# A two-layer decode kernel: another load order and other buffer places where a layer ends, and the output projection in pieces

## The chip, the cores and the metric

The kernel runs on one core of a Trainium2 chip. Its time is device microseconds of that core, from runs of the compiled program; the figure for the kernel before is the median of 10 runs. One further execution was taken with the hardware profiler; everything read from a profile or a trace here is from that one.

The engines' short names are those of the profile: PE is the matrix engine (its matmuls; PEld its weight loads), DVE the vector engine, ACT the scalar engine, SP the engine whose queue issues all loads. Sixteen DMA engines carry the loads.

## What is computed

```python
def _A_ref(x, k_cache, v_cache, wq, wo):          # B=2, one token, D=576, H=32, Sk=16384, Dh=128
    q = (x @ wq).reshape(B, Sq, H, Dh).transpose(0, 2, 1, 3)
    scores = einsum("bhqd,bhkd->bhqk", q, k_cache) * (Dh ** -0.5)
    p = softmax(scores, axis=-1)
    o = einsum("bhqk,bhkd->bhqd", p, v_cache)
    return o.transpose(0, 2, 1, 3).reshape(B, Sq, H * Dh) @ wo
...
x = A_x
x = x + _A_ref(_layernorm(x), k_cache, v_cache, wq, wo)
x = x + _B_ref(_layernorm(x), w1, w2, w3, w4)
x = x + _A_ref(_layernorm(x), k_cache, v_cache, wq, wo)
x = x + _B_ref(_layernorm(x), w1, w2, w3, w4)
```

`_B_ref` is a small MLP block: with one token its shifted branch leaves `x1 = x` (a product with zeros), and then `x1 + gelu(layernorm(x1) @ w3) @ w4`, with w3 of 576 x 4608 and w4 of 4608 x 576. Everything is bf16. Both layers read the same caches, 64 pairs of batch and head with 4 MB of K and 4 MB of V each: more than 1 GB in all, against a few MB of weights per layer.

## The kernel before

**Units.** A unit is one pair of batch and head. A layer is 64 units, then the MLP. Layer 1 takes the units in the order 0 to 63, layer 2 in the reverse, so that the last two units of layer 1 are the first two of layer 2 and stay in SBUF (`N_KEEP`, `kept`). In this document K[i] and V[i] are those of the i-th unit *in the order of the layer*, and "unit i" is that unit.

**A unit's work** (`attention`, L790). The K tile lies with 128 rows of the cache per column group. Half of it, in eight turns (`turn`, L656), is transposed by PE, copied out by ACT, and multiplied with the query on PE (`score`, L675). The other half is done by DVE: a product with the query's rows and a sum, eight pairs (`dots`, L687; L694 and L697). `row_max` and `unit_max` (L702, L712) give the maximum, `exps` (L720) the weights on ACT, and `weigh` (L731) is V times the weights on PE, 64 matmuls for each half of V. It runs one unit late: unit i's V is weighed inside unit i+1, around the end of its turns. PE's program has a loop over most units (`loops`, L796), with a body of two units: units 2 to 57 of layer 1 and 6 to 57 of layer 2; the others are written out.

**Places.** One SBUF tensor `buf` is cut in three thirds ("places" 0, 1, 2); a third has room for one K and one V (16384 bf16 per partition each). `place` (L328) tells which third a unit uses. In layer 1 units alternate between thirds 0 and 1; unit 63 uses third 2. In layer 2 the first five use 2, 0, 1, 2, 0, and from unit 5 on they alternate: odd units third 1, even ones third 2. The third that isn't used by units (2 in layer 1, 0 in layer 2) takes `wo`, in seven pieces of four heads and one "middle" piece of three heads (`want_wo`, L396); the last head has a tile of its own, `wolast`. wq for layer 1, and w2, use third 2 too; w3 and w4 use third 1 in layer 1 (that of unit 61) and third 0 in layer 2; wq for layer 2 comes into third 1, behind layer 1's w3 and w4.

**The queue of loads.** `plan` (L335) writes down all loads once, in one order: K[i], then V[i-1], from layer 2's unit 5 on as in layer 1; for layer 2's first five units K[i] and V[i] together. At the end come K[63], V[62], V[63], w3 in five row blocks and w4 in four pieces (`want_w34`, L375). The pieces of w4 have 5, 4, 2 and 1 parts; the first lies behind w3, the other three lie over w3's rows, so they wait until w3's matmuls have read them:

```python
                if c == 1:
                    at = base
```

`Arena` (L190) keeps this order. SP issues the loads one after the other, and each waits until the readers of what lay at its place are done. So K[i+2] waits for the dots of unit i where two thirds alternate, and a load that waits holds up all behind it.

**The output projection** (`project`, L748). For a range of heads: the softmax denominators by a matmul with ones, their sum and reciprocal on DVE, the normalized outputs `otn`, then one group of matmuls per head with `wo`, and a DVE add into `xa`. At the start of unit 59 the seven large pieces are projected in one go (140 matmuls), in layer 1 behind `shift_term` (L625); the middle piece at the end of unit 62, the last head after unit 63:

```python
            if i == last + 1:
                if l == 0:
                    self.shift_term()
                self.project_pieces(l, range(self.n_wo - 1))
```

PSUM tile `misc` is shared by these steps, the query rows and the unit maximum; `ops` has the result of weigh.

Of the kernel before, what the change touches and what calls it, by code (L numbers as in the profile page):

```python
# [4 lines left out]
ALU = mybir.AluOpType  # L5
# [228 lines left out]
class Decode:  # L234
# [2 lines left out]
    NKT = 3  # L237
    N_KEEP = 2
    N_MID = 3
    WO_PIECE = 4  # L240
    FJ = 3
    W4_PIECES = (5, 4, 2, 1)
# [85 lines left out]
    def place(self, l, i):  # L328


        if l == 0:
            return 2 if i == self.U - 1 else i % 2
        return (2, 0, 1, 2, 0)[i] if i < 5 else (2, 1)[i % 2]

    def plan(self):  # L335
        ring, B, H, D, KT, U = self.ring, self.B, self.H, self.D, self.KT, self.U
        unit = 2 * self.half
        self.order = [list(range(U)), list(reversed(range(U)))]
        self.kept = set(self.order[0][-self.N_KEEP:])

        def kv(kind, l, i, split=False):
            u = self.order[l][i]
            if l == 1 and u in self.kept:
                return
            b, hh = u % B, u // B
            src = {"K": self.K, "V": self.V}[kind][b, hh]
            pl = self.place(l, i)
            at = pl * self.place_n + {"K": 0, "V": unit}[kind]
            if split:
                ap = src.rearrange("(t p j) d -> t p (j d)", t=2, p=128)  # L350
                for h in range(2):
                    ring.want([(kind, l, u, h)], at + h * self.half, self.half,
                              [lambda e, v, h=h: e.dma_start(v, ap[h])])
            else:
                ap = src.rearrange("(p j) d -> p (j d)", p=128)
                ring.want([(kind, l, u, h) for h in range(2)], at, unit, [lambda e, v: e.dma_start(v, ap)],
                          sem=f"{kind}{pl}")
# [13 lines left out]

        def want_wq(l, p):
            rows("wq", l, self.wq, p * self.place_n + unit, last=p * self.place_n + 7 * unit // 8)

        def want_w34(l, p):  # L375
            base = p * self.place_n
            rows("w3", l, self.w3, base)
            at, a0 = base + (2 * KT - 1) * self.F // 2, 0
            for c, n in enumerate(self.W4_PIECES):
                m = n * self.FJ * D  # L380
                if c == 1:
                    at = base
# [3 lines left out]
                ring.want([("w4", l, c)], at, m,  # L386
                          [lambda e, v, ap=ap, n=n: e.dma_start(v.rearrange("p (a m) -> p a m", a=n), ap)])
# [13 lines left out]

        want_wq(0, 2)
        for l in range(2):
            wp = 2 - 2 * l
            early = 5 if l == 1 else 0
            gap = max(1, (U - 16) // self.n_wo)
            for i in range(U):
                kv("K", l, i, split=(l == 1 and i == 2))
                if i < early:
                    kv("V", l, i)  # L410
                elif i - 1 >= early:
                    kv("V", l, i - 1)
                j, r = divmod(i - 7, gap)
                if r == 0 and 0 <= j < self.n_wo:
                    want_wo(l, j, wp * self.place_n + (unit if j == self.n_wo - 1 else j * self.WO_PIECE * D))
                if l == 0 and i == 6:
                    want_w2(wp * self.place_n + 5 * unit // 4)
# [313 lines left out]
    def weigh(self, l, i, h):  # L731
        u = self.order[l][i]
        q = i % 2
        vt, res = self.ring.get(self.key("V", l, u, h))

        def f(pe):
            for j in range(self.TB):
                ins = pe.matmul(self.ops[q][:, 0:1], lhsT=vt[:, j * 128:(j + 1) * 128],  # L738
                                rhs=self.p[q][:, h * self.TB + j:h * self.TB + j + 1],
                                start=(h == 0 and j == 0), stop=(h == 1 and j == self.TB - 1))  # L740
            return ins
        self.pe(f, r=[*res, f"p{q}"], w=[f"P:ops{q}"])
        self.release("V", l, u, h)
        if h == 1:
# [3 lines left out]
    def project(self, l, h0, h1, parts):  # L748


        B, D, KT = self.B, self.D, self.KT
        u0, u1 = h0 * B, h1 * B
# [8 lines left out]
        self.dve(lambda v: v.tensor_tensor(out=self.otn[:, u0:u1], in0=self.o[:, u0:u1], in1=den, op=ALU.mult),  # L761
                 r=["den", "o"], w=["otn"])
        out = self.misc[:, 256:256 + KT * B]
        for first, n, w, res, after in parts:
            def f(pe, first=first, n=n, w=w):
                for j in range(n):
# [7 lines left out]
                                           in1=out.rearrange("p (t b) -> p t b", b=B), op=ALU.add),  # L774
                 r=["P:misc", "xa"], w=["xa"])

    def project_pieces(self, l, js):
# [6 lines left out]
        self.project(l, parts[0][0], parts[-1][0] + parts[-1][1], parts)  # L784

    def project_last(self, l):
        h = self.order[l][-1] // self.B
        self.project(l, h, h + 1, [(h, 1, self.wolast[:, :], ["wolast"], lambda: None)])

    def attention(self, l):  # L790
        U, NCP, NCH = self.U, self.NCP, self.NCH
        self.waiting = []
        self.query(l, 0)
        self.query_rows(l, 0)
        first, last = 2 + 4 * l, U - 6
        self.s.loops.append((l * U + first, (last - first) // 2, 2))  # L796
        for i in range(U):
            self.s.tag = l * U + i
            if i == U // 2:
                self.load_wo_last(l)  # L800
# [20 lines left out]
            while self.waiting:  # L821
                self.score()
            if i >= 1:
                self.weigh(l, i - 1, 1)
            if i == U - 2:
                self.project_pieces(l, [self.n_wo - 1])
            if i + 1 < U:
                self.query_rows(l, i + 1)
            self.row_max(l, i)
        self.s.tag = None  # L830
        self.unit_max(l, U - 1)
# [37 lines left out]
```

## Time and profile before

| | |
|---|---|
| median of 10 runs | 2591.03 us (2590.16 to 2591.62) |
| the profiled execution's own time | 2591.68 us |
| its span, first to last instruction | 2589.9 us |
| DVE busy | 1977.2 us, 76% |
| PE busy | 1537.1 us, 59% |
| ACT busy | 1110.2 us, 43% |
| HBM read | 1097.74 MB, 424 GB/s over the span |
| mean granted PE clock | 0.656 |

The page gives busy time, not need: an engine that waits for data isn't busy. Times inside the execution count from the span's start. A line such as L694 is a line of the kernel; the line of a load is that of the lambda which made it (L356: a whole K or V, L353: half of one, L370: rows of wq or w3, L387: a piece of w4, L400: a piece of wo). The page has a row per group of instructions, a row per group of loads with its size and the median time from issue to landing, and slices of the span; the trace gives the same for any stretch. A load has landed when all sixteen DMA engines have carried their share.

### The profile page before, as it was taken

What the parts mean: (1) busy time and instruction counts of PE and PEld (TensorE: products, weight loads), DVE (VectorE), ACT (ScalarE), POOL (GpSimd) and SP (SyncE); (2) the same over time, 40 slices, a digit from 0 to 9 for tenths busy, and PEclk for the clock granted to TensorE, in tenths of its full rate; (3) what the DMA queues carried; (4) which work ended last, traced back from release to release, by engine and by line L of the source; (5) the groups of instructions that cost most, each with busy time, mean ns of one, the idle gap of its engine ahead of it and who ended that gap; (6) DMA issues with size and microseconds to landing.
All of it is one profiled execution on the core that took longest, in us unless ns stands there. A gap on an engine that the chain in (4) does not pass through costs nothing.

```text
span 2589.9 us, 75423 instructions
## 1 busy us (share of the span) xinstructions
PE 1537.1 (59%) x34519; PEld 1447.8 (56%) x34519; DVE 1977.2 (76%) x2775; ACT 1110.2 (43%) x1809; POOL 0.8 (0%) x10
## 2 busy tenths in 40 slices
PE   5656555655565555557567655556555655566565
PEld 4555555555555555546566655555555555555565
DVE  5877787778777777877759877877777777778775
ACT  3434444444444344434335444434443444444442
POOL 0000000000000000000000000000000000000000
PEclk8666666666666666666656666666666666667665
DMA  9999999999999999999998999999999999999998
GB/s 412 431 428 431 429 432 432 430 432 430 431 430 432 431 433 428 434 431 399 424 391 362 433 431 430 430 430 433 431 430 432 432 430 430 430 433 432 432 420 342
DMA packets 51322, 1099.05 MB, mean 424 GB/s; under 512 B 4820, under 2 KB 13080, under 8 KB 16792
## 3 DMA queue, kind: packets, MB, share of 16 engines
q1 hardware_dynamic: 51224, 1097.76, 99.1%
q8 instruction: 59, 0.97, 0.1%
q14 instruction: 39, 0.32, 0.0%
HBM read 1097.74 MB, written 0.00 MB: 424 GB/s over the span
## 4 chain that ended last, share of the span: by engine, by line
DMA 54%; DVE 38%; PE 7%; issue 1%; SPq 0%; ACT 0%; DVEq 0%
DMA buf<-in_A_k_cache_dram 50%; DVE sd L697 23%; DVE prod L694 13%; PE tps L665 4%; DMA buf<-in_A_v_cache_dram 2%; PE misc L715 2%; DVE small L717 1%; DMA buf<-in_A_wq_dram 1%; PE misc L575 0%; PE ops L738 0%; DMA buf<-in_B_w_dram 0%; PE sps L539 0%; SPq L370 0%; PE misc L505 0%; DVE small L709 0%
## 5 line engine op out<-in xcount | busy, mean ns | idle before, releaser
L669 ACT ACTIVATE ktsb<-tps 128x1024 bf16<-128x1024 bf16 x1024 | 1003.7, 1028 | 862.3 <-PE tps L665 857.1
L697 DVE TENSOR_REDUCE sd<-prod 128x8 f32<-128x1024 bf16 x1024 | 1249.3, 1220 | 35.5
L665 PE MATMUL tps<-ident,buf 128*128 128x128 bf16 x8192 | 829.3, 268 | 669.2 <-DMA buf<-in_A_k_cache_dram 666.8
L665 PEld LDWEIGHTS tps<-ident,buf 128*128 128x128 bf16 x8192 | 673.4, 123 | 698.7 <-DMA buf<-in_A_k_cache_dram 688.4
L694 DVE TENSOR_TENSOR prod<-buf,qb 128x1024 bf16<-128x1024 bf16 x1024 | 697.8, 681 | 11.3 <-DMA buf<-in_A_k_cache_dram 10.4
L738 PE MATMUL ops<-p,buf 128*128 128x1 bf16 x16384 | 467.7, 165 | 194.7 <-DMA buf<-in_A_v_cache_dram 181.5
L738 PEld LDWEIGHTS ops<-p,buf 128*128 128x128 bf16 x16384 | 448.8, 102 | 206.3 <-DMA buf<-in_A_v_cache_dram 189.8
L682 PE MATMUL sps<-qcur,ktsb 128*128 128x1 bf16 x8192 | 350.4, 166 | 93.2 <-ACT ktsb L669 84.5
L717 DVE TENSOR_REDUCE small<-misc 128x1 f32<-128x128 f32 x128 | 37.4, 292 | 478.8 <-PE misc L715 478.8
L682 PEld LDWEIGHTS sps<-qcur,ktsb 128*128 128x128 bf16 x8192 | 313.3, 102 | 133.5 <-ACT ktsb L669 131.2
L653 ACT ACTIVATE qb<-misc 128x128 bf16<-128x128 f32 x128 | 35.5, 278 | 519.6 <-PE misc L650 519.6
L715 PE MATMUL misc<-identS,small 128*128 128x128 f32 x256 | 95.6, 477 | 41.8 <-DVE small L709 41.8
L715 PEld LDWEIGHTS misc<-identS,small 128*128 128x128 f32 x256 | 69.7, 332 | 45.1 <-DVE small L709 36.1
L726 ACT ACTIVATE p<-sps,small 128x64 bf16<-128x64 f32 x128 | 40.7, 318 | 19.1 <-DVE small L717 19.1
L726 ACT ACTIVATE p<-sd,small 128x64 bf16<-128x64 f32 x128 | 45.5, 355 | 0.0
L645 ACT ACTIVATE qcur<-qt 128x1 bf16<-128x1 bf16 x128 | 29.3, 229 | 19.3 <-DVE qt L582 19.3
L650 PE MATMUL misc<-ident,qcur 128*128 128x128 bf16 x128 | 34.3, 268 | 1.6 <-ACT qcur L645 1.1
L705 DVE TENSOR_REDUCE small<-sps 128x1 f32<-128x64 f32 x128 | 27.4, 214 | 0.0
L726 ACT ACTIVATION_READ_ACCUMULATOR p<-sps,small 128x1 f32 x128 | 27.2, 212 | 0.0
L707 DVE TENSOR_REDUCE small<-sd 128x1 f32<-128x64 f32 x128 | 26.6, 208 | 0.0
L726 ACT ACTIVATION_READ_ACCUMULATOR p<-sd,small 128x1 f32 x128 | 26.5, 207 | 0.0
L745 DVE COPY o<-ops 128x1 f32<-128x1 f32 x128 | 19.0, 149 | 9.5 <-PE ops L738 9.5
(74 smaller groups left out, 158.0 us busy)
## 6 DMA issues: line engine op xcount, KB each, us to landing
buf<-in_A_v_cache_dram SPq DMA_DIRECT2D x126, 4096.0 KB, 31.8
buf<-in_A_k_cache_dram SPq DMA_DIRECT2D x125, 4096.0 KB, 22.5
buf<-in_B_w_dram SPq DMA_DIRECT2D x8, 1152.0 KB, 29.3
buf<-in_A_wq_dram SPq DMA_DIRECT2D x8, 1024.0 KB, 10.5
buf<-in_A_wo_dram SPq DMA_DIRECT2D x14, 576.0 KB, 32.8
buf<-in_B_w_dram SPq DMA_DIRECT2D x2, 2160.0 KB, 36.4
buf<-in_A_k_cache_dram SPq DMA_DIRECT2D x2, 2048.0 KB, 16.7
buf<-in_B_w_dram SPq DMA_DIRECT2D x2, 1728.0 KB, 7.9
```

Of the source, the lines that this page charges most:

```text
L645: self.act(lambda a: a.activation(out=self.qcur[:, q:q + 1], in_=self.qt[:, u:u + 1], func=ACT.Copy), r=["qt"], w=[f"qcur{q}"])
L650: self.pe(lambda pe: pe.matmul(self.misc[:, 0:128], lhsT=bcast(self.qcur[:, q:q + 1], 128), rhs=self.ident[:, :], start=True, stop=True), ...
L653: self.act(lambda a: a.activation(out=self.qb[q][:, :], in_=self.misc[:, 0:128], func=ACT.Copy), r=["P:misc"], w=[f"qb{q}"])
L665: ins = pe.transpose(self.tps[b][:, j * 128:(j + 1) * 128], kt[:, (j0 + j) * 128:(j0 + j + 1) * 128], self.ident[:, :])
L669: self.act(lambda a: a.activation(out=self.ktsb[k][:, :, :].rearrange("p a b -> p (a b)"), in_=self.tps[b][:, :], func=ACT.Copy), r=[f"P:t ...
L682: ins = pe.matmul(self.sps[sp][:, col:col + 1], lhsT=self.ktsb[k][:, j, :], rhs=self.qcur[:, sp:sp + 1], start=True, stop=True)
L694: self.dve(lambda v: v.tensor_tensor(out=self.prod[d][:, :, :], in0=k3, in1=bcast_mid(self.qb[q][:, :], self.CH), op=ALU.mult), r=[*res, f ...
L697: self.dve(lambda v: v.tensor_reduce(out=self.sd[q][:, o:o + self.CH], in_=self.prod[d][:, :, :], axis=AX.X, op=ALU.add), r=[f"prod{d}"], ...
L715: self.pe(lambda pe: pe.matmul(self.misc[:, 128:256], lhsT=bcast(self.m[:, q:q + 1], 128), rhs=self.identS[:, :], start=True, stop=True), ...
L717: self.dve(lambda v: v.tensor_reduce(out=self.bias[:, q:q + 1], in_=self.misc[:, 128:256], axis=AX.X, op=ALU.max, negate=True), r=["P:misc ...
L726: self.act(lambda a, c0=c0, c1=c1, src=src, part=part: a.activation(out=self.p[q][:, c0:c1], in_=src, func=ACT.Exp, bias=self.bias[:, q:q ...
L738: ins = pe.matmul(self.ops[q][:, 0:1], lhsT=vt[:, j * 128:(j + 1) * 128], rhs=self.p[q][:, h * self.TB + j:h * self.TB + j + 1], start=(h ...
```

## The change

The units' places: unit 63 of layer 2 goes to third 0 (layer 1's stays in 2). Layer 2's units 0 to 11 rotate over the three thirds; from unit 12 on they alternate as before. The load of `wo` in layer 2 starts at unit 13, not 7.

The order of loads: K[63] comes ahead of V[61], V[62] and V[63], in halves, and V[63] is in halves too; so is V[2] of layer 2. In layer 2, w3 and the first piece of w4 go to third 1 (that of unit 61) and w4's later three pieces to third 2 (that of unit 62); in layer 1 all stay where they were. The middle piece of `wo` moves to the end of its third, and w2 from 5/4 to 4/4 of a unit.

The projection: `project` is taken apart into `normalizers`, `normalize` and `project`. The seven large pieces are used at the ends of units 57 to 60 in groups of two, two, two and one; `shift_term` is at the end of unit 60. The middle piece is used in unit 63's fourth turn, behind the weigh of unit 61, which moves there from unit 62. In layer 2's units 1 to 4 the weigh of the unit before runs after the sixth turn, and its exponentials one turn sooner. At the layer's end the last head's denominators come ahead of the last weigh, and the last output is normalized straight from PSUM. PE's loops now run over units 2 to 55 and 12 to 55.

```diff
     def place(self, l, i):
+        if i == self.U - 1:
+            return 2 - 2 * l
         if l == 0:
-            return 2 if i == self.U - 1 else i % 2
-        return (2, 0, 1, 2, 0)[i] if i < 5 else (2, 1)[i % 2]
+            return i % 2
+        return (2, 0, 1)[i % 3] if i < self.ROT else (2, 1)[i % 2]
...
-        def want_w34(l, p):
+        def want_w34(l, p, p1):
...
                 if c == 1:
-                    at = base
-                assert at + m <= (p + 1) * self.place_n
+                    assert at <= base + self.place_n
+                    at = p1 * self.place_n
...
-            gap = max(1, (U - 16) // self.n_wo)
+            wo_at = 7 if l == 0 else self.ROT + 1
+            gap = max(1, (U - 8 - wo_at) // self.n_wo)
             for i in range(U):
-                kv("K", l, i, split=(l == 1 and i == 2))
+                kv("K", l, i, split=(l == 1 and i == 2) or i == U - 1)
                 if i < early:
-                    kv("V", l, i)
-                elif i - 1 >= early:
+                    kv("V", l, i, split=(l == 1 and i == 2))
+                elif early <= i - 1 < U - 3:
                     kv("V", l, i - 1)
-                j, r = divmod(i - 7, gap)
+                j, r = divmod(i - wo_at, gap)
                 if r == 0 and 0 <= j < self.n_wo:
-                    want_wo(l, j, wp * self.place_n + (unit if j == self.n_wo - 1 else j * self.WO_PIECE * D))
+                    want_wo(l, j, wp * self.place_n + (2 * unit - self.N_MID * D if j == self.n_wo - 1
+                                                            else j * self.WO_PIECE * D))
...
-            kv("V", l, U - 1)
-            want_w34(l, 1 if l == 0 else 0)
+            for i in range(U - 3, U):
+                kv("V", l, i, split=i == U - 1)
+            want_w34(l, 1, 1 if l == 0 else 2)
...
+    def normalizers(self, u0, u1):
         dps = self.misc[:, 320:320 + 2 * (u1 - u0)]
         self.pe(lambda pe: pe.matmul(dps, lhsT=bcast(self.cone[:, :], 128),
...
+    def normalize(self, u0, u1, o, res):
+        self.dve(lambda v: v.tensor_tensor(out=self.otn[:, u0:u1], in0=o, in1=self.den[:, u0:u1], op=ALU.mult),
+                 r=["den", res], w=["otn"])
...
-        first, last = 2 + 4 * l, U - 6
+        first, last = (2, self.ROT)[l], U - 8
...
-            if i == last + 1:
-                if l == 0:
-                    self.shift_term()
-                self.project_pieces(l, range(self.n_wo - 1))
+            early = l == 1 and 1 <= i <= 4
             dv = list(range(NCP, NCH))
             for c in range(NCP):
...
-                if i >= 1 and c == 4:
+                if i >= 1 and c == (3 if early else 4):
                     self.exps(l, i - 1)
...
+                if early and c == 5:
+                    self.weigh(l, i - 1, 0)
+                    self.weigh(l, i - 1, 1)
+                if i == U - 1 and c == 3:
+                    self.weigh(l, i - 2, 0)
+                    self.weigh(l, i - 2, 1)
+                    self.normalize(*mid, self.o[:, slice(*mid)], "o")
+                    self.project_pieces(l, [self.n_wo - 1])
-            if i >= 1:
+            now = i >= 1 and not early and i != U - 2
+            if now:
                 self.weigh(l, i - 1, 0)
...
             self.row_max(l, i)
+            if i == last + 1:
+                self.normalizers(*most)
+                self.normalize(*most, self.o[:, slice(*most)], "o")
+            if last + 1 <= i <= last + 4 and pieces:
+                self.project_pieces(l, [pieces.pop(0) for _ in range(min(2, len(pieces)))])
+            if l == 0 and i == last + 4:
+                self.shift_term()
+            if i == U - 2:
+                self.normalizers(*mid)
...
         self.unit_max(l, U - 1)
         self.exps(l, U - 1)
-        for h in range(2):
-            self.weigh(l, U - 1, h)
-        self.project_last(l)
+        self.normalizers(h * self.B, (h + 1) * self.B)
+        other = self.order[l][-2]
+        self.normalize(other, other + 1, self.o[:, other:other + 1], "o")
+        self.weigh(l, U - 1, 0)
+        self.weigh(l, U - 1, 1)
+        q = (U - 1) % 2
+        self.normalize(u, u + 1, self.ops[q][:, 0:1], f"P:ops{q}")
+        self.project(h, h + 1, [(h, 1, self.wolast[:, :], ["wolast"], lambda: None)])
```

More of the change, by code (lines that the diff above doesn't have):

```diff
@@ L239 @@
     N_MID = 3
+    ROT = 12
     WO_PIECE = 4
@@ L405, in plan @@
             early = 5 if l == 1 else 0
[L406 removed]
+            wo_at = 7 if l == 0 else self.ROT + 1
+            gap = max(1, (U - 8 - wo_at) // self.n_wo)
             for i in range(U):
[L408 removed]
+                kv("K", l, i, split=(l == 1 and i == 2) or i == U - 1)
                 if i < early:
[L410 to L411 removed]
+                    kv("V", l, i, split=(l == 1 and i == 2))
+                elif early <= i - 1 < U - 3:
                     kv("V", l, i - 1)
[L413 removed]
+                j, r = divmod(i - wo_at, gap)
                 if r == 0 and 0 <= j < self.n_wo:
[L415 removed]
+                    want_wo(l, j, wp * self.place_n + (2 * unit - self.N_MID * D if j == self.n_wo - 1
+                                                            else j * self.WO_PIECE * D))
                 if l == 0 and i == 6:
[L417 to L419 removed]
+                    want_w2(wp * self.place_n + unit)
+            for i in range(U - 3, U):
+                kv("V", l, i, split=i == U - 1)
+            want_w34(l, 1, 1 if l == 0 else 2)
             if l == 0:
@@ L743, in weigh @@
         self.release("V", l, u, h)
-        if h == 1:
+        if h == 1 and i < self.U - 1:
             self.dve(lambda v: v.tensor_copy(out=self.o[:, u:u + 1], in_=self.ops[q][:, 0:1]),
                      r=[f"P:ops{q}"], w=["o"])
-    def project(self, l, h0, h1, parts):
-        B, D, KT = self.B, self.D, self.KT
-        u0, u1 = h0 * B, h1 * B
+    def normalizers(self, u0, u1):
         dps = self.misc[:, 320:320 + 2 * (u1 - u0)]
@@ L760, in project @@
         self.dve(lambda v: v.reciprocal(out=den, in_=den), r=["den"], w=["den"])
-        self.dve(lambda v: v.tensor_tensor(out=self.otn[:, u0:u1], in0=self.o[:, u0:u1], in1=den, op=ALU.mult),
-                 r=["den", "o"], w=["otn"])
+    def normalize(self, u0, u1, o, res):
+        self.dve(lambda v: v.tensor_tensor(out=self.otn[:, u0:u1], in0=o, in1=self.den[:, u0:u1], op=ALU.mult),
+                 r=["den", res], w=["otn"])
+    def project(self, h0, h1, parts):
+        B, D, KT = self.B, self.D, self.KT
         out = self.misc[:, 256:256 + KT * B]
@@ L775, in project, with columns @@
                  r=["P:misc", "xa"], w=["xa"])
+    def columns(self, l, js):
+        u0 = min(self.wo_piece(l, j)[0] for j in js) * self.B
+        u1 = max(self.wo_piece(l, j)[1] for j in js) * self.B
+        return u0, u1
     def project_pieces(self, l, js):
@@ L783, in project_pieces @@
         parts.sort(key=lambda p: p[0])
[L784 to L788, printed above, removed]
+        self.project(parts[0][0], parts[-1][0] + parts[-1][1], parts)
     def attention(self, l):
@@ L794, in attention @@
         self.query_rows(l, 0)
-        first, last = 2 + 4 * l, U - 6
+        first, last = (2, self.ROT)[l], U - 8
+        assert first < last and (last - first) % 2 == 0
+        pieces = list(range(self.n_wo - 1))
+        most, mid = self.columns(l, pieces), self.columns(l, [self.n_wo - 1])
+        assert len(pieces) <= 8
         self.s.loops.append((l * U + first, (last - first) // 2, 2))
@@ L822, in attention @@
                 self.score()
-            if i >= 1:
+            if now:
                 self.weigh(l, i - 1, 1)
-            if i == U - 2:
-                self.project_pieces(l, [self.n_wo - 1])
             if i + 1 < U:
@@ L829, in attention @@
             self.row_max(l, i)
+            if i == last + 1:
[7 more added lines that the diff above has]
+                self.normalizers(*mid)
         self.s.tag = None
+        u, h = self.order[l][-1], self.order[l][-1] // self.B
         self.unit_max(l, U - 1)
         self.exps(l, U - 1)
-        for h in range(2):
-            self.weigh(l, U - 1, h)
-        self.project_last(l)
+        self.normalizers(h * self.B, (h + 1) * self.B)
[6 more added lines that the diff above has]
+        self.project(h, h + 1, [(h, 1, self.wolast[:, :], ["wolast"], lambda: None)])
 def bass_interleave_layers__mha_block_cached__mixer_s_mlp__decode_kernel(
```

## The prediction

> **What bounds the kernel now.** I read the page's slices first. The first two lines below are the busy share of the DMA engines and the GB/s that they moved, in 40 slices of 64.7 us; the third is SP's queue.
>
> ```profile
> DMA  9999999999999999999998999999999999999998
> GB/s 412 431 428 431 429 432 432 430 432 430 431 430 432 431 433 428 434 431 399 424 391 362 433 431 430 430 430 433 431 430 432 432 430 430 430 433 432 432 420 342
> q1 hardware_dynamic: 51224, 1097.76, 99.1%
> ```
>
> The kernel is bound by loading. Bytes don't change, so a gain can only come from the slices below 430: numbers 19 to 22 (the turn from layer 1 to layer 2) and the last two. I then cut those stretches into windows (columns: stretch, length, busy us of PE, PEld, DVE, ACT, POOL, granted clock, DMA share, GB/s):
>
> ```profile
> 1204.00:1212.00 8.00, 4.23 (x43) 3.90 (x43) 6.94 (x13) 2.73 (x4) 0.00 (x0) 0.50 0.58 209
> 1296.00:1300.00 4.00, 3.25 (x122) 3.16 (x119) 0.23 (x1) 0.42 (x2) 0.00 (x0) 0.50 0.67 209
> 1336.00:1352.00 16.00, 12.56 (x259) 12.14 (x259) 14.80 (x21) 8.62 (x14) 0.00 (x0) 0.61 0.82 317
> 1352.00:1410.00 58.00, 42.20 (x884) 40.33 (x885) 53.38 (x76) 31.39 (x52) 0.00 (x0) 0.63 1.00 427
> 1410.00:1420.00 10.00, 5.75 (x159) 5.49 (x157) 9.39 (x14) 3.65 (x6) 0.00 (x0) 0.58 0.21 54
> 2568.00:2577.00 9.00, 5.72 (x167) 5.57 (x167) 1.99 (x14) 1.00 (x4) 0.00 (x0) 0.50 0.37 122
> ```
>
> Five dips. A dip is a mean over 16 engines, and they don't run level: in the trace each transfer raises its semaphore 16 times, and for V[59] of layer 1 the first rise is at 1204.0 us, the last at 1213.8. One DMA engine lags the others by 9.9 us. A transfer has landed when the last engine is done, so only idle time of **the last engine** is lost. SP's timeline gives issues, the line's own view the time to landing; here the last three issues ahead of the deep dip, and below them the landings of 1182 (K[60] and V[59], layer 1), of 1385 (K[6] and V[5], layer 2) and of 1417.86 (K[7]).
>
> ```profile
> 1384.83 0.33 SPq L356 DMA_DIRECT2D buf<-in_A_k_cache_dram  x1
> 1385.20 0.43 SPq L356 DMA_DIRECT2D buf<-in_A_v_cache_dram  x1
> 1417.86 0.33 SPq L356 DMA_DIRECT2D buf<-in_A_k_cache_dram  x1
> ...
> DMA to landing us min/median/max: 22.5/27.1/31.8
> ...
> DMA to landing us min/median/max: 17.0/21.6/26.2
> ...
> DMA to landing us min/median/max: 13.6/13.6/13.6
> ```
>
> K lands 22.5 us after issue and V 31.8 after an issue 0.37 later, so 4096 KB take the last engine **9.7 us**. An issue into idle engines needs 2.0 us before data flows: 13.6 - 9.7 - 1.9 (lag of that last engine). With this, dip by dip (issue + landing time):
> - 1204: V[59] lands 1182.08 + 31.8 = 1213.9; K[61], issued 1208.01, lands 1223.6, 9.7 later. Lost: 0.
> - 1296: first w4 piece lands 1265.57 + 35.0 = 1300.6, the second (1728 KB, due 4.1) at 1304.8. Lost: 0.
> - 1336: V[2] lands 1320.87 + 18.4 = 1339.2; K[3] 1335.35 + 15.9 = 1351.2, so 12.0 for 9.7: 2.3. V[3], issued 1349.19, lands 1363.0: 11.7 for 9.7: 2.0.
> - 1410: V[5] lands 1411.4; K[7] 1431.5, so 20.1 for 9.7: **10.4**.
> - 2568: first w4 piece lands 2539.20 + 37.9 = 2577.1, the last 2576.10 + 9.9 = 2586.0: 9.0 for 3024 KB, due 7.2: 1.8 lost. These pieces wait for w3's matmuls, as SP's waits say (L387, longest 35.1 us).
>
> ```profile
> SPq L387 <- PE sps L539: 68.0, 4, 35.1
> ```
>
> **Other thirds for layer 2's units 0 to 11.** K[7] shared a third with K[5], and waited for dots of unit 5. Now it shares with K[4]. DVE finishes K units there every 16.5 us (K issues at 1335.35, 1351.80, 1368.31, 1384.83), so unit 4 is done at 1401.3. Walk the last engine from V[2] at 1339.2: K[3] to 1348.9, V[3] 1358.6, K[4] 1368.3, V[4] 1378.0, K[5] 1387.7, K[6] 1397.4, V[5] 1407.1, K[7] **1416.8**, if each issue is 2.0 us ahead. V[3] needs unit 0's weigh, which moves into unit 1 after the sixth transposes (1340.9 to 1342.1 in the old trace); 128 matmuls at 1.74 per 64 plus a stall of 1.4 seen there end it at 1345.6 to 1347.0, +2.0 against 1348.9. K[6] needs 1384.8 + 2.0 against 1387.7, K[7] 1403.3 against 1407.1, K[8] (unit 5) 1419.9 against V[6] at 1426.5. All fit, the tightest by about 0 and 0.9. So K[7] lands 14.7 us earlier than 1431.5, the three losses. Later rows in the queue follow directly; at unit 12 the two-thirds rotation starts, DVE's 16.5 against DMA's 19.4 per unit having rebuilt the queue, and the later wo pieces move the same bytes. Lower end: if V[3] or K[6] are late, 2 to 4 us stay.
>
> **w4's later pieces in another third.** They wait for dots of unit 62 instead of w3's matmuls in layer 2; SP issues them straight behind w3. Gain 1.8. Cover: after V[63] lands, the work until w4's last piece is needed is second half of weigh 1.75, normalize 0.2, last projection with its stall 2.0, to w3 6.1, w3 4.7, gelu 2.0, three w4 pieces 2.2 + 1.8 + 1.0 = 21.7; w3 and w4 (5184 KB each) take 24.6. DMA stays last, by 2.9 us; beyond that a stall costs its length. The 3.9 us from the last landing to the end stay. Layer 1 keeps its wait (place 1), which cost nothing.
>
> **Last K ahead of the last Vs, V halves.** Same bytes. SP now stops at K[63] until unit 60's projection (PE is done about 2 us ahead of DVE's unit 60, whose end K[62] needs anyway), and at V[63]'s second half until the middle projection in unit 63's fourth turn: about 1270 in layer 1 (K[62] lands 1243.0, unit 62 is done 16.4 later as unit 58 was after its K, 1259.5, then a unit maximum and four dots). The last engine has V[61], V[62] and half of V[63] until 1277.0, so 5 us of spare; if gone, w3 and w4 queue behind, a us for a us, in each layer. Unit 63's dots end some 3 us earlier, the two halves of the last weigh and the last denominators off the tail; this gains nothing while loads are last. Here a rule speaks against: the Trainium skill's page "DMA: Bandwidth & Descriptors", "Latency and other measured facts", puts a fixed cost of about 2 us on a DMA, mostly the receipt. There are five more DMAs, so the rule read as time would take 10 us off my gain. The row: layer 2's split K[2] half lands 1307.97 + 16.7 = 1324.65, behind wq at 1319.8, 4.9 for half of 9.7. In a full queue the fixed cost doesn't show: 0.
>
> **Projection spread.** 140 matmuls (3.89 us) and shift (0.92) left one block, in which unit 59's dots slipped some 7 us, to 40, 40, 40 and 20 at the ends of units 57 to 60 (1.1 us each), with 0.8 + 0.3 + 0.5 + 0.2 for denominators once. At those ends PE waits for K some 3 us; and a K issue may slip 12.7 us (22.5 - 9.7) before the last engine idles. Cost 0. Gain 0 too, as the 1204 dip was not on the last engine.
>
> **More code.** PE's loops run units 2 to 55 and 12 to 55 of the layers instead of 2 to 57 and 6 to 57: ten more units written out. Before, about 24 units' code (bodies among them) took 59 fetch packets of 16 KB, so 24 more. Their row between 1189 and 1304:
>
> ```profile
> q8 instruction: 14, 0.23, 0.8%
> ```
>
> 0.8% of 16 engines over 115 us is 14.7 us, 1.05 each. Bounds: 0 if all fall on engines with slack, 25 if all on the last. In that stretch the last engine lost 0.9 for 14 packets, so they spread: 24 x 1.05 / 16 = 1.6. About 0.9 of K[3]'s 2.3 looks like fetches too, and stays. I charge **2.5**. The skill's "Runtime: NRT & Kernel Launch", "Instruction fetch mechanics", has the fetch as mostly hidden: by the rule 0, a time 2.5 lower. I take the row.
>
> **Sum.** 14.7 + 1.8 - 2.5 = 14.0 us. Span 2589.90 to 2575.9; outside it stay 1.78 (2591.68 for that execution); against the median 2591.03: **2577.0**.
>
> **Rivals.**
> - *All dips come back* (10%): the mean over engines is what counts. Missing against 427: 4.1 + 2.0 + 4.1 + 8.7 + 6.4 = 25.3; time about 2566. For: the page's 40 slices. Against: landings 9.7 apart through two dips.
> - *A new wait keeps part* (15%): V[63]'s second half or V[3]/K[6] late by 4 to 8 us; 2582 to 2587. For: in-order SP, a spare of 5 and 0. Against: the walk above.
> - *Fetches fall on the last engine* (6%): 24 x 1.05 = 25 us against 16.5 gained: about 2600. It decides from 16 of 24 packets on that engine. For: that engine's lag grows about 1 us per 120 us in steady loops, so something does single it out. Against: 0.9 for 14.
> - *Forecast* (69%): 2573 to 2581.
>
> Under 0.2% (5.2 us) isn't told from no change. Faster: forecast, the first, most of the second: 0.89; same 0.05; slower 0.06. The range takes in the forecast's own and most of the second.
>
> **What would show it.** Right: no window of zero GB/s near 1410; K[7] landing near 1417 to 1419; the three late w4 pieces issued right behind the first; q8 packets near 83; last landing 3.9 us ahead of the end. Wrong: SP waiting long on the middle projection with DMA share under 1; transfers 11 us apart in units 0 to 12 of layer 2; a tail in which PE, not w4's landing, is last.

## The result, and the profile after

| | before | after |
|---|---|---|
| median of the runs | 2590.95 us (28 runs, 2589.74 to 2591.63) | 2577.57 us (8 runs, 2577.43 to 2578.56) |
| profiled execution, its span | 2591.68, 2589.9 us | 2577.70, 2575.8 us |
| mean granted PE clock | 0.656 | 0.653 |

The ratio is 0.9949, with a 95% interval of 0.994 to 0.9958: 13.4 us are gone. On the page after, these are the rows of the slices and of the DMA queues:

```profile
DMA  9999999999999999999999999999999999999998
GB/s 414 430 427 432 432 432 431 432 429 429 433 432 431 430 432 432 432 429 428 406 403 424 430 428 431 431 432 429 431 432 430 431 432 430 431 432 432 428 428 358
...
q1 hardware_dynamic: 51944, 1097.76, 99.6%
q8 instruction: 80, 1.31, 0.2%
q14 instruction: 39, 0.32, 0.0%
```

The slice with 362 GB/s is gone, and the last but one is at 428. Slices 20 and 21, around the turn to layer 2, still show 406 and 403. The same stretches as before, cut into windows (for the tail the same work, which ends some 14 us earlier):

```profile
1204.00:1212.00 8.00, 7.17 (x106) 6.77 (x107) 5.34 (x7) 6.49 (x11) 0.00 (x0) 0.71 1.00 428
1296.00:1300.00 4.00, 1.48 (x54) 1.39 (x51) 1.26 (x4) 0.49 (x2) 0.00 (x0) 0.50 0.98 339
1336.00:1352.00 16.00, 13.21 (x259) 12.54 (x259) 14.80 (x21) 7.78 (x13) 0.00 (x0) 0.50 0.98 394
1352.00:1410.00 58.00, 45.77 (x908) 44.13 (x909) 53.34 (x76) 33.10 (x55) 0.00 (x0) 0.56 1.00 427
1410.00:1420.00 10.00, 6.05 (x141) 5.64 (x138) 8.94 (x14) 3.05 (x4) 0.00 (x0) 0.50 1.00 428
2554.00:2563.00 9.00, 5.99 (x167) 5.76 (x167) 1.74 (x11) 0.93 (x5) 0.00 (x0) 0.50 1.02 415
```

These dips are filled or nearly so: 54 GB/s became 428 at 1410, 122 became 415 in the tail, 209 became 428 at 1204. If every filled dip counted, the gain would be about 25 us, the first rival; it is 13.4. The means over sixteen engines say where the transfers changed, not what they are worth.

What K[7] does shows the largest piece. First SP's timeline, with the issues of K[6], V[5], K[7] and V[6], then the time from issue to landing that the view of the load's line gives for K[7]:

```profile
1384.29 0.33 SPq L359 DMA_DIRECT2D buf<-in_A_k_cache_dram  x1
1384.66 0.42 SPq L359 DMA_DIRECT2D buf<-in_A_v_cache_dram  x1
1400.81 0.33 SPq L359 DMA_DIRECT2D buf<-in_A_k_cache_dram  x1
1401.19 0.43 SPq L359 DMA_DIRECT2D buf<-in_A_v_cache_dram  x1
```

```profile
DMA to landing us min/median/max: 19.7/19.7/19.7
```

K[7] is issued 16.5 us behind K[6], where it had been 33.0, and lands at 1400.8 + 19.7 = 1420.5 on the last engine, 11.0 us earlier than before. Landings on the last engine, from the sixteen rises of each transfer's semaphore in the trace:

| landed, us | before | after | difference |
|---|---|---|---|
| V[2], layer 2 | 1339.24 | 1338.67 | 0.6 |
| K[3] | 1351.21 | 1349.64 | 1.6 |
| K[4] | 1372.58 | 1370.56 | 2.0 |
| V[5] | 1411.39 | 1409.40 | 2.0 |
| K[7] | 1431.48 | 1420.47 | 11.0 |
| V[63] | 2559.39 | 2546.85 | 12.5 |
| last piece of w4 | 2586.04 | 2571.98 | 14.1 |

The two profiled executions are 14.0 us apart, the medians 13.4.

From V[2] to K[4] the engine's steps are 10.97, 11.04 and 9.88 us, and to K[7] 11.07, against 9.7 for the bytes. The new stop of SP at the layer's end is long, but not late. SP's waits:

```profile
SPq L356 <- PE misc L581: 63.4, 3, 31.0
...
SPq L390 <- PE sps L545: 21.5, 2, 20.9
```

The first is the stop at V[63]'s second half. In layer 1 that half is issued at 1270.56, and the half ahead of it lands on the last engine at 1277.89, 7.3 us later; in layer 2 it is 2534.55 against 2541.93, 7.4 us. Less the 2.0 us that an issue into idle engines takes, 5.3 us were to spare. Both second halves land 4.9 us behind the first, without a gap. The mean over the engines does dip while SP stands there, in both layers, where it had not before:

```profile
1266.00:1270.00 4.00, 1.46 (x55) 1.38 (x53) 3.81 (x6) 0.00 (x0) 0.00 (x0) 0.50 0.69 287
2530.00:2534.00 4.00, 1.46 (x55) 1.38 (x52) 3.80 (x6) 0.00 (x0) 0.00 (x0) 0.50 0.69 295
```

Only engines that are ahead of the last one are idle in these.

### The profile page after: what moved, and what is told of

Its sections match the earlier page's. It is cut to its first block, busy times and chain, and to the rows that moved or that the text cites. A ratio compares the mean times of both kernels' runs of the same rounds, so it can differ in the third digit from the quotient of the medians.

```text
span 2575.8 us, 75345 instructions
## 1 busy us (share of the span) xinstructions
PE 1544.3 (60%) x34519; PEld 1456.0 (57%) x34519; DVE 1978.1 (77%) x2781; ACT 1110.4 (43%) x1809; POOL 0.8 (0%) x10
## 4 chain that ended last, share of the span: by engine, by line
DMA 54%; DVE 38%; PE 6%; SPq 1%; issue 1%; ACT 0%; DVEq 0%
DMA buf<-in_A_k_cache_dram 51%; DVE sd L703 24%; DVE prod L700 13%; PE tps L671 4%; DMA buf<-in_B_w_dram 2%; PE misc L721 2%; DVE small L723 1%; SPq L390 1%; DMA buf<-in_A_wq_dram 1%; SPq L373 0%; PE misc L581 0%; DVE small L715 0%; DVE small L713 0%; DVE small L711 0%; DVE den L763 0%
## 5 line engine op out<-in xcount | busy, mean ns | idle before, releaser
L700 DVE TENSOR_TENSOR prod<-buf,qb 128x1024 bf16<-128x1024 bf16 x1024 | 697.9, 682 | 11.1 <-DMA buf<-in_A_k_cache_dram 10.1
L545 PE MATMUL sps<-xn,buf 128*128 128x2 bf16 x544 | 16.7, 166 | 14.2 <-DMA buf<-in_A_wq_dram 9.7
## 6 DMA issues: line engine op xcount, KB each, us to landing
buf<-in_A_v_cache_dram SPq DMA_DIRECT2D x123, 4096.0 KB, 31.9
```

Of the source, the lines that this page charges most:

```text
L700: self.dve(lambda v: v.tensor_tensor(out=self.prod[d][:, :, :], in0=k3, in1=bcast_mid(self.qb[q][:, :], self.CH), op=ALU.mult), r=[*res, f ...
```

## The experiments

Each ran beside the kernel before on the same chip, whose medians there were 2590.94 to 2591.27. Unless said otherwise an edit is made to the changed kernel.

**The old rotation, and nothing else undone.**

```diff
-    ROT = 12
+    ROT = 5
...
-            wo_at = 7 if l == 0 else self.ROT + 1
+            wo_at = 7
...
-        first, last = (2, self.ROT)[l], U - 8
+        first, last = (2, 6)[l], U - 8
```

> The changed kernel with layer 2's first units in the thirds of before (2, 0, 1, 2, 0, then 1 and 2 in turn), wo from unit 7 and PE's loop from unit 6, as before. Theory (only idle time of the last DMA engine counts): K[7] again waits for the dots of unit 5, some 10.4 us are lost there as before, less about 1 us for six units' code that is no longer fetched: about 2587. Rival (the empty stretch only shifts work, and the queue makes it up later): 2577 to 2579.

Measured 2588.82 us, ratio 0.9991 [0.9981, 1.0]. The rotation is worth 11.2 us. Windows and SP's timeline of this kernel:

```profile
1410.00:1420.00 10.00, 5.24 (x136) 4.92 (x132) 8.87 (x14) 2.91 (x4) 0.00 (x0) 0.66 0.23 70
```

```profile
1417.12 0.33 SPq L359 DMA_DIRECT2D buf<-in_A_k_cache_dram  x1
```

K[7] waits again for the dots of unit 5, and the step on the last engine from V[5] to K[7] is 21.4 us, where it is 11.1 with the rotation.

**The rotation alone**, put into the kernel before.

```diff
+    ROT = 12
...
-        return (2, 0, 1, 2, 0)[i] if i < 5 else (2, 1)[i % 2]
+        return (2, 0, 1)[i % 3] if i < self.ROT else (2, 1)[i % 2]
...
-            gap = max(1, (U - 16) // self.n_wo)
+            wo_at = 7 if l == 0 else self.ROT + 1
+            gap = max(1, (U - 9 - wo_at) // self.n_wo)
...
-                j, r = divmod(i - 7, gap)
+                j, r = divmod(i - wo_at, gap)
...
-        first, last = 2 + 4 * l, U - 6
+        first, last = (2, self.ROT)[l], U - 6
```

> The kernel before with one edit: layer 2's units 0 to 11 rotate over the three thirds, with wo from unit 13 and PE's loop from unit 12. No earlier weigh, no other order, no spread projection. Theory (the rotation is the change's gain, the earlier weigh adds 2): 10.4 us off, and 6 units' code more at 0.17 us per fetch packet (the no_loops run's 32 us over 190 packets), 2.2 on: 2583; with what no_rotation lost against the changed kernel (11.2), 2580. Rival (the rotation needs the earlier weigh or the spread projection to work): 2587 or more.

Measured 2581.64 us, ratio 0.9964 [0.995, 0.9978]: 9.3 us of the 13.4. K[7] lands at 1420.47, as in the changed kernel. The other 4.1 us are not there: V[63] lands at 2548.86, 2.0 later, and the last piece of w4 27.9 us behind it instead of 25.1. (The profiled execution's span, 2580.7 us, is about 1 us above that of its fellows, so these two differences add up to more than 4.1.)

**w4's later pieces over w3 again**, the rest changed.

```diff
-            want_w34(l, 1, 1 if l == 0 else 2)
+            want_w34(l, 1, 1)
```

> The changed kernel with w4's later pieces of layer 2 back over w3's rows, so that they wait for w3's matmuls. The prediction's term: +1.8, so 2579.4. Rival (in the changed kernel w3's matmuls start 10.6 us after V[63] lands instead of 13.0, so the pieces are issued early enough for the last DMA engine, and the term is covered by the other order): 2577.6 to 2578.

Measured 2577.60 us, ratio 0.9948 [0.9931, 0.9965]. That third is worth 0.0 us in the changed kernel, not 1.8. Here the second piece of w4 waits for w3's matmuls and is issued at 2559.04; the first lands at 2564.18, and the second 4.22 later, hardly more than the 4.1 of its bytes. It is issued 5.1 us ahead of that landing; before it was 2.3 (2574.73 against 2577.07), and the step was 5.58.

**The projection in one block**, at the start of unit 59 as before.

```diff
+            if i == last + 3:
+                if l == 0:
+                    self.shift_term()
+                self.normalizers(*most)
+                self.normalize(*most, self.o[:, slice(*most)], "o")
+                self.project_pieces(l, pieces)
...
-            if last + 1 <= i <= last + 4 and pieces:
-                self.project_pieces(l, [pieces.pop(0) for _ in range(min(2, len(pieces)))])
```

> The changed kernel with the seven large pieces projected in one block at the start of unit 59, as before. Theory (unit 59 slips 7 us, the last DMA engine has 12.7 us queued): 2577.6, same. Rival (dips of the mean over engines count: 4.1 us in layer 1, 1.5 in layer 2): 2583.

Measured 2577.93 us, ratio 0.9948 [0.9932, 0.9965]: 0.4 us. The window of the dip at 1204 is at 289 GB/s in this kernel (209 before, 428 with the spread), but the last engine's step across it is 9.73 us, as without a dip. Filling this dip was worth next to nothing.

**The old order of the last K and Vs**, halves kept.

```diff
-                elif early <= i - 1 < U - 3:
+                elif early <= i - 1:
...
-            for i in range(U - 3, U):
+            for i in range(U - 1, U):
```

> The changed kernel with K[63] behind V[61] and V[62] behind K[63], the order of before, everything else as changed. Theory (the order only moves PE's tail by 2 to 3 us, and w4's landing is last by 2.9): 2577.6 to 2578. Rival (the order keeps DMA or the tail from waiting): 2580 to 2583.

Measured 2577.39 us, ratio 0.9947 [0.9931, 0.9964]: 0.2 lower, within what repeats.

**The whole layer end of before**: K[63] and V[63] whole, in the old order, the middle projection at the end of unit 62, the last head's denominators behind the weigh; only w4's third and the spread projection stay. And the same with w4's later pieces over w3.

```diff
-                kv("K", l, i, split=(l == 1 and i == 2) or i == U - 1)
+                kv("K", l, i, split=(l == 1 and i == 2))
...
-                kv("V", l, i, split=i == U - 1)
+                kv("V", l, i)
...
-            now = i >= 1 and not early and i != U - 2
+            now = i >= 1 and not early
...
                 self.normalizers(*mid)
+                self.normalize(*mid, self.o[:, slice(*mid)], "o")
+                self.project_pieces(l, [self.n_wo - 1])
...
```

```diff
-            want_w34(l, 1, 1 if l == 0 else 2)
+            want_w34(l, 1, 1)
```

> The changed kernel with the whole layer end of before: K[63] behind V[61], no halves, unit 61 weighed in unit 62 and the middle piece projected there, the last denominators behind the last weigh. w4's later pieces keep their own third, the projection of the large pieces stays spread. Theory: loads stay last, w4 doesn't wait for anything: 2577.6 to 2578. Rival (the new layer end carries part of the gain by itself): 2579.4 or more.

> As old_tail, and w4's later pieces of layer 2 over w3's rows, as before. Theory (either of the two, a shorter way from V[63] to w3 or an own third for w4, hides the wait for w3's matmuls; without both it is back): w3 starts 13 us after V[63] lands as before, 1.6 to 1.8 us lost: 2579.2 to 2579.6. Rival (w4's wait never cost anything, the 1.8 us of before were chance of that execution): 2577.6 to 2578.

Measured 2577.16 us, ratio 0.9947 [0.993, 0.9963], and 2577.24 us, ratio 0.9946 [0.9929, 0.9963]. The second missed: I had thought that the shorter work behind V[63] was what made w4's third worthless, so that with the old layer end over it w4 would cost some 2 us again. It costs nothing. My theory fell. The rows of PE's timeline around w3's first matmuls show what differs. The last field is the idle time ahead of a row and what ended it. The kernel before:

```profile
2565.98 0.29 PE L575 MATMUL misc<-otn,wolast 128*128 128x2 bf16 x5 [2.27 <-issue]
2572.41 1.12 PE L539 MATMUL sps<-xn,buf 128*128 128x2 bf16 x36 [1.51 <-DVE xn L523]
```

The rotation alone:

```profile
2555.12 0.65 PE L740 MATMUL ops<-p,buf 128*128 128x1 bf16 x19 [3.08 <-issue]
...
2563.28 1.12 PE L541 MATMUL sps<-xn,buf 128*128 128x2 bf16 x36 [1.51 <-DVE xn L525]
```

The old layer end with w4 over w3, in the changed kernel:

```profile
2551.63 0.29 PE L581 MATMUL misc<-otn,wolast 128*128 128x2 bf16 x5 [0.65 <-DVE otn L766]
...
2558.06 1.12 PE L545 MATMUL sps<-xn,buf 128*128 128x2 bf16 x36 [1.51 <-DVE xn L529]
```

The changed kernel:

```profile
2551.06 0.29 PE L581 MATMUL misc<-otn,wolast 128*128 128x2 bf16 x5 [0.26 <-DVE otn L766]
...
2557.48 1.16 PE L545 MATMUL sps<-xn,buf 128*128 128x2 bf16 x36 [1.51 <-DVE xn L529]
```

"<-issue" is a stall that no data explains. There is one of 2.27 us behind V[63] before, and one of 3.08 in the rotation alone; in the other two PE waits 0.65 and 0.26 us, for DVE. The trace has each packet of PE's code with its start and length, and these stalls end just behind one. The changed kernel's 1.38 us, behind V[63]'s first half, is the same:

| kernel | stall of PE, us | packet of code in or just ahead of it | packet's end to PE's going on |
|---|---|---|---|
| before | 2563.71 to 2565.98 | 2563.61 to 2564.71 | 1.27 |
| rotation alone | 2552.04 to 2555.12 | 2552.78 to 2553.88 | 1.24 |
| changed | 2541.82 to 2543.20 | 2540.74 to 2541.83 | 1.37 |

So PE waits for its own code there, as far as times can tell. From the kernel before to the rotation alone the layer end's work is the same and six more units are written out, and the stall is in another place and longer. From V[63]'s landing to w3's first matmul the four kernels take 13.0, 14.4, 11.2 and 10.6 us. In the three that have w4's pieces over w3, the second piece is then issued 2.3, 1.0 and 4.2 us ahead of the first one's landing, and its step is 5.58, 6.21 and 4.19.

**w4's third where PE is late.** If so, w4's own third is worth something in the kernel with the stall of 3.08 us. So, to the rotation alone:

```diff
-                if c == 1:
-                    at = base
+                if c == 1:
+                    at = p1 * self.place_n
...
-            want_w34(l, 1 if l == 0 else 0)
+            want_w34(l, 1 if l == 0 else 0, 1 + l)
```

> rotation_alone with w4's later pieces of layer 2 in third 2 besides. In rotation_alone PE waits 3.1 us for its own code behind V[63], w3's matmuls start 14.4 us after V[63] lands, w4's second piece is issued late and the last piece lands 27.9 after V[63] instead of 25.1. Theory (w4's own third is worth something only where PE's code is late, and is worth 2 to 3 us here; PE is then last itself by up to 1 us): 2578.8 to 2579.8. Rival (the tail's loss has another cause): 2581.6.

Measured 2579.60 us, ratio 0.9955 [0.9938, 0.9972]: 2.0 us lower than the rotation alone. The stall of 3.08 us is still in its timeline, but the last piece of w4 now lands 25.1 us behind V[63], not 27.9. So w4's own third is worth 2.0 us with a late PE, 0 without: insurance, not a gain of its own.

**The weigh of layer 2's units 1 to 4 back behind the turns.**

```diff
-            early = l == 1 and 1 <= i <= 4
+            early = False
```

> The changed kernel without the earlier weigh in layer 2's units 1 to 4 (it runs at the unit's end, as before). Theory: V[3] is issued near 1348.5 instead of 1345.0, too late for a queue that ends near 1349.6 less the 2 us that an issue into idle engines takes: 0.5 to 2 us lost: 2578.1 to 2579.6. Rival (the fetches of written-out code set the landing there anyway): 2577.6.

Measured 2579.68 us, ratio 0.9956 [0.9939, 0.9973]: the early weigh is worth 2.1 us. SP's timeline in this kernel, then in the changed one:

```profile
1334.71 0.33 SPq L359 DMA_DIRECT2D buf<-in_A_k_cache_dram  x1
1348.31 0.33 SPq L359 DMA_DIRECT2D buf<-in_A_v_cache_dram  x1
```

```profile
1334.73 0.33 SPq L359 DMA_DIRECT2D buf<-in_A_k_cache_dram  x1
1344.95 0.33 SPq L359 DMA_DIRECT2D buf<-in_A_v_cache_dram  x1
```

V[3] is issued 3.4 us later and yet lands at the same time (1360.67 against 1360.68), as its step in the changed kernel is a long one too; K[4] lands 1.1 later on the last engine, K[7] at the same time again (1420.47), V[6] 1.1 later, V[63] 1.9 (2548.77 against 2546.85). Lone steps of the last engine are about 1 us longer, now in one of the two kernels and now in the other, so two traces are too few. From V[2] to K[4], landing to landing, the three kernels that rotate without the early weigh (this one, the rotation alone, and that with w4's third) take 32.6 to 33.0 us, the six with it and DVE's code unchanged 31.3 to 31.9. From V[2] to V[63] it is 1209.7 to 1210.1 against 1207.0 to 1208.3. So the 2.1 us are real and lie in layer 2, and a good 1 us of them is lost by K[4]; where the rest is lost isn't shown. With the 9.3 us of the rotation alone and the 2.0 that the late PE cost there, they make up the 13.4.

**PE's loops away**, so that all of its code is written out: the fetches measured by themselves.

```diff
-        self.s.loops.append((l * U + first, (last - first) // 2, 2))
```

> The changed kernel with PE's loops taken away, all 128 units written out: 98 units more, at 2.15 packets of 16 KB each some 210 more fetches. By the row (1.05 us each, spread over 16 DMA engines): +14 us, 2591; with the 1.4 us that one packet shifts a DMA engine in the trace, +18, 2596. Rival (fetching is hidden): 2577.6. Rival (all on one DMA engine): above 2750.

Measured 2609.81 us, ratio 1.0072 [1.0055, 1.0089]: 32.2 us more for 190 more packets, **0.17 us a packet**. The page's row:

```profile
q8 instruction: 270, 4.42, 0.7%
```

This was more than the 14 or 18 us of my two forecasts. The way in which the sixteen engines stand apart shows why. For V[61] of layer 1, the times of its semaphore's sixteen rises from the first one on, in us, in this kernel and in the changed one:

```
PE written out  0.0 0.1 0.5 1.0 1.0 1.2 1.4 1.4 10.3 10.3 10.4 10.6 10.6 10.8 10.8 10.9
changed kernel  0.0 0.0 0.0 0.7 1.1 1.5 2.5  4.1  4.5  4.5  4.6  4.6  4.7  4.7  4.8 10.7
```

Eight engines run level, and the other eight run level about 9 us behind: PE's fetches go to **eight engines, not sixteen**. 0.7% of 16 engines over 2608 us is 292 us, 1.08 a packet; 190 x 1.08 / 8 = 26 of the 32.2 us (the share is rounded, so 24 to 28). A fetch holds a load up for more than its own time: from one landing to the next mostly one engine alone moves against the others, by about 1.5 us (between the landings at 878.75 and 888.49, from 8.3 to 9.8 behind the first). With 1.5 a packet the same sum gives 36 us, so the 32.2 lie between the two counts. Why it is more than 1.08 isn't shown. "Mostly hidden", as the Trainium skill's page "Runtime: NRT & Kernel Launch" has it ("Instruction fetch mechanics"), doesn't hold here, where the queue of loads fills 98.9% of the engines' time.

**A loop for DVE too.** In the changed kernel's row above one engine alone stands at 10.7 us, with the next at 4.8. DVE's program is written out as well. The packets of q14 come in two rows: in layer 1 of the kernel before one every 120 us or so (898.5, 1019.6, 1138.4), and one every 180 (800.6, 977.7, 1164.1). At each of the first row the last engine's lag grows by 1.0 us, though a packet takes 0.32: 2.1 us at 73 us, 6.0 at 707, 9.9 at 1142. At each of the second row another engine's lag grows by 0.7. I took the first row for DVE's. So DVE goes into the same loops. The small copy of weigh's result moves from DVE to ACT, so that DVE's order repeats; what is computed stays.

```diff
-                def run(eng, items=plan[e], loops=self.loops if e == "tensor" else ()):
+                def run(eng, items=plan[e], loops=self.loops if e in ("tensor", "vector") else ()):
...
-            self.dve(lambda v: v.tensor_copy(out=self.o[:, u:u + 1], in_=self.ops[q][:, 0:1]),
+            self.act(lambda a: a.activation(out=self.o[:, u:u + 1], in_=self.ops[q][:, 0:1], func=ACT.Copy),
```

> The changed kernel with DVE's program in the same loops as PE's (98 of 128 units), and the copy of weigh's result into o moved from DVE to ACT, as its column differs from unit to unit. Theory (the last DMA engine falls behind by about 1 us per 120 us because DVE's code pages are fetched through it): its lag stays small in layer 1, until an engine that fetches PE's or ACT's code is the last: some 5 us off in layer 1 and 1 in layer 2, 2571 to 2573. Rival (that engine is slower by itself): 2577.6 to 2579.

Measured **2572.00 us**, ratio 0.9926 [0.991, 0.9943], 5.6 us below the changed kernel and the lowest of all. The page:

```profile
q8 instruction: 80, 1.31, 0.2%
q14 instruction: 25, 0.20, 0.0%
```

Fourteen packets of 8 KB fewer: the row of 120 us is gone from the steady units, the other is still there (577.7, 751.5, 914.3), and no run shows whose code that is. At V[62] of layer 1 the last engine is 5.7 us behind the first instead of 10.6; V[62] lands at 1267.87 instead of 1272.99. A row that the page rounds to 0.0% cost 5.6 us, since its load falls on the engine that decides. The copy's move alone was not run, but the lone engine's lag goes with the packets.

**A shorter rotation on top**: nine units, so that fewer of PE's are written out.

```diff
-    ROT = 12
+    ROT = 9
...
-        return (2, 0, 1)[i % 3] if i < self.ROT else (2, 1)[i % 2]
+        return (2, 0, 1)[i % 3] if i < self.ROT else (1, 2)[i % 2]
...
-            want_w34(l, 1, 1 if l == 0 else 2)
+            want_w34(l, 1 + l, 1)
...
-        first, last = (2, self.ROT)[l], U - 8
+        first, last = (2, self.ROT + 1)[l], U - 8
```

> As vector_loop, with only nine units of layer 2 rotating (then odd units third 2, even ones third 1; PE's and DVE's loops from unit 10; w3 and w4's later pieces at each other's third). Two units' code less: some 4 packets at 0.17 us, 0.7 us off against vector_loop. Rival: K[10], which waits for the dots of unit 8, comes late for the queue, up to 2 us on.

Measured 2572.27 us, ratio 0.993 [0.9913, 0.9946]: 0.3 more, no difference. Five packets fewer (75) should have been worth 0.8; too little to be seen, or taken back by less time to rebuild the queue.

## Why the prediction was right, step by step

The time was foretold within 0.6 us, and the mechanism holds: only idle time of the last engine counts, and it was lost mainly where K[7] waited for a third. But the sum came out partly because terms that were off cancelled.

- **Dip by dip.** Borne out. The 1204 dip was called 0, and filling it is worth 0.4. The second rival's hold-ups did not come: SP's stop in layer 1 ended at 1270.56, where the prediction had about 1270. The third rival needed 16 of 24 packets on the last engine.
- **The three losses, 14.7 us.** Mechanism right, size off. K[7] landed at 1420.5, not 1416.8. The walk had 9.7 us a step; three steps took 1.3 more. One is K[7]'s own, at 11.07, where no issue was late: it was issued 8.6 us ahead of V[5]'s landing. V[3] was issued at 1344.95, 0.7 earlier than the earliest that was worked out, and its step took 11.04 all the same. I put these three down to fetches by their size alone; with the weigh put back the long step moved on by one, as K[7]'s is 9.94 there and V[6]'s 11.02. At the end the rotation measured 11.2 us, with the 13 packets that it adds already taken off, and the early weigh 2.1, of which a good 1 was followed.
- **The fetch charge, 2.5 us.** The term that was mis-sized. It stood on fetches spreading over sixteen engines; they go to eight. By the 0.17 us a packet of the written-out kernel the 21 new ones (59 to 80; foretold 83) cost 3.6, an estimate. The row was closer than the rule's 0. The 0.9 us that the last engine lost between 1189 and 1304, from which the prediction took it that PE's packets spread, fell on V[61] (step 10.64), where packets of q14 came (1243.7 and 1252.2), so it was most likely not PE's code. The third rival had the right suspicion on the wrong engine: what singles one engine out is DVE's code, not PE's.
- **w4's third, 1.8 us.** The term came true by luck, as far as the cause goes. The tail from V[63] to the last piece of w4 shrank from 26.65 to 25.13 us, 1.5. But with the pieces over w3 again it is as short. What had held them was PE's stall of 2.27 us in that place, which the prediction's own list contained as "with its stall", priced as if it stayed.
- **What cancelled.** As an estimate: the rotation without the charge for its 13 packets (11.2 + 2.2) and the early weigh (2.1) give 15.5 where the sum had 14.7; the tail gave 1.5, not 1.8; the fetches took 3.6, not 2.5. That is 13.4 again: the first came out 0.8 us better than foretold, the other two 1.4 worse.
- **Order, halves, projection, five more DMAs: 0.** As said: 2577.39 with the old order, 2577.16 with the whole old layer end, 2577.93 with the block. The old layer end has four DMAs fewer, two in each layer, and is 0.4 us faster at most, not the 8 that a fixed 2 us each would make: the fixed cost that the Trainium skill's page "DMA: Bandwidth & Descriptors" ("Latency and other measured facts") puts on a DMA shows in no run with a full queue.
- **The signs.** No hole near 1410, a tail that ends 3.9 us behind the last landing, 80 packets: right. Of w4's late pieces only the first followed straight behind (2537.92); the others were issued at 2549.30 and 2556.90 and still landed one behind the other, 2.08 and 1.06 us apart. K[7] at 1420.5 is outside its 1417 to 1419. Two signs of being wrong came too: three steps of 11 us (K[3], V[3], K[7]), and a DMA share of 0.69 while SP waited for the middle projection, which cost nothing, as the last engine had 5.3 us left.

Open: why a fetch holds a load up for longer than its own time, the second microsecond of the early weigh, and which of the lone steps belong to which fetch.

## What to carry to other kernels

In a kernel bound by loading, follow the landings of the slowest DMA engine one by one; a dip of the mean bandwidth may cost its whole length (10 us at 1410) or next to nothing (at 1204), and the mean can't tell which. Written-out code isn't free there: it is loaded by the same engines, so loop the steady part on every engine whose code is long, not only on the one with the most instructions. A load that waits for an engine's last reads is hostage to any stall of that engine, so give it a place of its own even if it gains nothing today.

## What the runs showed of the hardware

- PE's code came over eight of the sixteen DMA engines: with 190 more packets those eight stand about 9 us behind the others.
- DVE's code burdened one engine alone, by about 1 us a packet of 8 KB: in layer 1 of the changed kernel that engine lands 10.6 us behind the first, with DVE looped the last one 5.7 (2577.57 to 2572.00 with 14 packets fewer).
- PE's stalls of 2.27, 3.08 and 1.38 us in the tails of three kernels each ended 1.2 to 1.4 us behind a packet of its code, and from the kernel before to the rotation alone, with the same work there, the stall moved.
